# Thirty-four narrow unread matmuls in three waits of TensorE, and the two copies of a partial sum traded between ScalarE and VectorE

## The chip, the core and the metric

The kernel is one program on one NeuronCore of a Trainium2 chip. The metric is device microseconds from the start to the end of one execution, as median over several. TensorE (PE in the profile) multiplies into PSUM, VectorE (DVE) and ScalarE (ACT) read PSUM and write SBUF, GpSimd (POOL) works on SBUF and issues the weight loads, SyncE (SP) issues the other loads and the stores. The engines run their own instruction lists in order and meet only through semaphores.

## The reference

Two layers follow each other. The first is a gated recurrence over 5056 tokens for 4 sequences (B) and 256 channels (D); the second is a mixture of 8 experts with 4 slots each, over all 20224 tokens.

```
sig = 1 / (1 + exp(-f_logit));  f = lb + (1 - lb) * sig;  i = 1 - f
for t in range(S):  h = f[:, t] * h + i[:, t] * x[:, t];  y[:, t] = h

logits = y @ phi                                   # 20224 x 32 slots
d = exp(logits), divided by its sum over the tokens
slot_input = d.T @ y                               # 32 x 256
slot_out = relu(slot_input @ w1[e]) @ w2[e]        # each expert its 4 slots, F = 1024
c = exp(logits), divided by its sum over the slots
out = c @ slot_out
```

Nothing of `out` can be computed before `slot_out`, and `slot_out` needs all tokens and all weights.

## The kernel before

**First stage.** The tokens are cut into groups of 512 (`n_grp` = 10), and a unit `n` (0 to 39) is one group of one sequence. For each unit the tokens are loaded (`load`, SyncE), the gate is computed (`gate`, ScalarE, L235), gate times input is formed (`enter`, GpSimd, L246), both are transposed to channels by TensorE (`s_to_channels`, `u_to_channels`, L261, L267, and L255 and L258 for the odd group), the decay is made by ScalarE (`decay`, L295, L302), the recurrence is run by VectorE (`scan`, L313, two instructions a unit), the result is transposed back (`to_tokens`, L326) and copied out of PSUM by VectorE or ScalarE (`keep_tokens`, L345). Per group the logits are formed (`logits`, L359), exponentiated (`exps`, L368), transposed (`weights_to_tokens`, L380, copied by L383) and multiplied with the tokens into the sum `slot_ps` (`slots`, L410).

**Order.** The order of the work is written out by hand: the loop over `n` (L461 to L567) emits each unit's steps, and each engine runs its own in that order. GpSimd also issues the loads of the weights (`load_w`, L137 and L147) at the units that `W_AT` names, in program order behind its own work.

**Fillers.** `idle(k)` (L177) emits `k` float32 matmuls into `slot_bank[:, 1]`, the second half of the PSUM bank whose first half is `slot_ps`. Nothing reads that half. `spin(dst, k, w)` (L150) does the same with bfloat16 operands. At units 35 and 36 (`n_unit - 5`, `n_unit - 4`) there are `idle(2)` calls; unit 37 has none.

**Second stage.** `slot_ps` is copied out (L587), scaled to `sin` (L602, L603), goes through the first weights (L621) and ReLU (L626, L628), is transposed (L636) and laid into `hid` and `wide` (L645, L653), and goes through the second weights: experts 0 to 3 in L658, experts 4 to 7 in the loop over `j` and `fc` at L702, eight matmuls (L705) an expert. GpSimd clears `wide` (L572) before L653 writes it. The last expert's weights (`w_t`, tile of `w2_sb[7]`) come in three pieces: `fc` 0 to 3, 4 and 5, 6 and 7.

**The partial sum.** The sum over all but the last four `fc` of the last expert is kept in `so_ps`, the rest in `sb_ps`. When `so_ps` is complete, it is scaled and copied twice: to bfloat16 (`part_b`, ScalarE, L712) and to float32 (`part`, VectorE, L713). `part_b` feeds two matmuls of `early_part` (L699), which stand on TensorE between `fc` 5 and `fc` 6; their sums `early_ps` give the first two rows of the output of one sequence (`early`, L734) without waiting for `slot_out`. `part` is added to the rest in one VectorE instruction that makes `slot_out`:

```
nc.vector.scalar_tensor_tensor(slot_out, sb_ps, rcs, part, ALU.mult, ALU.add)
```

**Third stage.** All output tokens are formed from `slot_out` (L755) or its two-sequence form `slot_bd` (L738, L811), scaled by VectorE (L745) and ScalarE (L749), and stored by SyncE (L736, L785, L802, L817, L834).

Of the kernel before, what the change touches and what calls it, by code (L numbers as in the profile page):

```python
# [13 lines left out]
ACT = mybir.ActivationFunctionType  # L14
# [4 lines left out]
def kernel(  # L19
# [10 lines left out]
    nc = tc.nc  # L30
    B, S, D = x.shape
    E = moe_w1.shape[0]
    F = moe_w1.shape[2]
    NS = moe_phi.shape[1]
# [7 lines left out]
    n_unit = n_grp * B  # L42
# [27 lines left out]
    ident = consts.tile([P, P], BF16, name="ident")  # L70
# [13 lines left out]
    def rep_constants(b):  # L84
        blk = ident_f[ds(b * NS, NS), ds(b * NS, NS)]
        nc.gpsimd.tensor_copy(rep[ds(b * NS, NS)], blk.unsqueeze(1).broadcast_to([NS, B, NS]))  # L86
# [45 lines left out]
    w1_sb = [wts.tile([P, DC, F], BF16, name=f"w1_sb{e}") for e in range(E)]  # L132
# [29 lines left out]
    with tc.tile_pool(name="sp2", bufs=3) as sp2, \  # L162
# [9 lines left out]
        slot_bank = pslot.tile([P, 2, D], F32, name="slot_ps")  # L172
# [4 lines left out]
        def idle(k, first=False):  # L177
            if first:
                for i in range(2):
                    nc.tensor.matmul(slot_bank[:, 1, ds(0, P)], ident, ident,  # L180
                                     start=True, stop=False, skip_group_check=True)
            for _ in range(k):
                nc.tensor.matmul(slot_bank[:, 1], ident_f, wide_rep,  # L183
                                 start=False, stop=False, skip_group_check=True)
        xs, fs, sts, uts, pss, psus, hs, hps, hts, lgs, ets = ({} for _ in range(11))

        def long(n):
# [81 lines left out]
        def s_to_channels(n):  # L269
            if n % 2 == 0:  # L270
                pss[n // 2] = psp.tile([P, 2, P, R], F32, name="sp", tag="sp")
            to_channels(n, pss[n // 2][:, n % 2], sts[n // 2][:, n % 2],
                        sts[n // 2][:, 0, R3])
# [142 lines left out]
        def unit(f, m):  # L416
            if 0 <= m < n_unit:
                f(m)
# [60 lines left out]
        for n in range(n_unit):  # L479
            if n < SINGLE - 2:  # L480
                if n:
                    unit(to_tokens, n - 1)
                    unit(u_to_channels, n + 1)
                s_to_channels(n + 2)
                if n + 3 < SINGLE:
                    gate(n + 3, 1)
                decay(n + 2, 1)
                if n + 3 == SINGLE:
                    gate(n + 3)
                if n % 2 == 0:  # L490
                    unit(load, n + AHEAD)
                unit(enter, n + 3)
                rep_constants(n)
            else:
                end = n >= n_unit - 6
                if n % 2 == 0:
                    unit(load, n + AHEAD)
                    if n == SINGLE - 2:
                        to_tokens(n - 1)
                        keep_tokens(n - 1)  # L500
                    if not end and n >= SETTLED:
                        unit(gate, n + 4)
                else:
                    unit(decay, n + 1)
                    if n < SETTLED:
                        gate(n + 3)
                    if n == n_unit - 5:
                        gate(n + 3)
                        exps(odd - 1)
                if not end and n != n_unit - 7:  # L510
                    group(exps, n - 2)

                unit(enter, n + 3)
                for _ in range(W_AT.get(n, 0)):
                    load_w(w_next[0])
                    w_next[0] += 1

                if n == n_unit - 2:
                    unit(u_to_channels, n + 1)
                if n != SINGLE - 2:  # L520
                    unit(to_tokens, n - 1)
                if n == n_unit - 2:
                    keep_tokens(n - 1)
                if n % 2 == 0:
                    unit(s_to_channels, n + 2)
                    unit(s_to_channels, n + 3)
                if n != n_unit - 2:
                    unit(u_to_channels, n + 1)
                if n in (n_unit - 5, n_unit - 4):
                    idle(2)  # L530
                elif n == SINGLE - 2:
                    idle(1, True)
                elif n < n_unit - 4 and n % (2 * B) in (1, 5, 6, 7):
                    idle(2 if n in (6, 7) else 1)
                if n == n_unit - 2:
                    tail = psp.tile([P, 2, G], F32, name="tail", tag="sp")
                    sums = tail[:, 0]
                    rs_ps = sums[:, ds(0, n_grp * R * B)].rearrange(
                        "p (q b) -> p q b", b=B)
                    late_ps, odd_ps = (  # L540
                        tail[:, 1].bitcast(BF16)[:, ds(i * R * P, R * P)].rearrange(
                            "p (r s) -> p r s", r=R) for i in range(2))
                    logits(odd)
                    exps(odd)
                    slots(odd - 2)
                elif not end and long(n - 1):
                    if n % B == 0:
                        g = (n - 1) // (2 * B) * 2
                        for i in range(2):
                            logits(g + i, [2, 3] if n % (2 * B) == 0 else [0, 1])  # L550
                elif not end:
                    group(logits, n - 1)
            if n == n_unit - 1:
                odd_weights()
                logits(last, [0, 1, 2])

            unit(scan, n)
            if n not in (SINGLE - 2, n_unit - 2):
                unit(keep_tokens, n - 1)
            if n == n_unit - 3:  # L560
                weights_to_tokens(odd - 1, nc.scalar.copy)
            elif not n >= n_unit - 6:
                group(weights_to_tokens, n - 3)
                batch(slots, n - 4, 0)
                batch(slots, n - 4, 1)
                if n > 2 * B and n % (2 * B) == 3:
                    idle(1)  # L567
# [22 lines left out]
        for o in range(DC):  # L590
            nc.tensor.matmul(sin_ps[:, o], slot_v[:, o], rep[:, 0],
                             start=True, stop=True, skip_group_check=True)
        spin(slot_bank[:, 1], 6, D)

    with tc.tile_pool(name="ew", bufs=1) as ew, \
# [18 lines left out]
        for q in range(E // Q):  # L614
            hi = ew.tile([P, F], BF16, name=f"hi{q}")
            for k in range(2):
                hi_ps = (psu.tile([P, H], F32, name="hi_ps", tag="up") if q == 0 else
                         pbig.tile([P, H], F32, name="hi_ps", tag=f"hi_ps{k}"))
                for o in range(DC):
                    for j in range(Q):  # L620
                        nc.tensor.matmul(hi_ps[ds(j * NS, NS)], sin[:, o],  # L621
                                         w1_sb[q * Q + j][:, o, ds(k * H, H)],
                                         start=(o == 0), stop=(o == DC - 1),
                                         skip_group_check=True)
# [6 lines left out]
        rcs = ew.tile([P, 1], F32, name="rcs")  # L631
# [24 lines left out]
        for e in range(Q):  # L656
            for fc in range(FC):
                nc.tensor.matmul(so4_ps[ds(fc % 4 * NS, NS), :], hid[:, fc, e],  # L658
                                 w2_sb[e][:, fc],
                                 start=(e == 0 and fc < 4),  # L660
                                 stop=(e == Q - 1 and fc >= FC - 4),
                                 skip_group_check=True)
# [10 lines left out]
        so_ps = pm.tile([P, D], F32, name="so_ps", tag="pm")  # L673
# [3 lines left out]
        for i in range(0, n_late, 2):  # L677
            g_ps = psu.tile([P, 2, 2, P], F32, name="g_ps", tag="up")
            for k in range(2):
                nc.tensor.matmul(g_ps[:, k], hi_v[tail_b, FC - n_late + i + k], ex[tail_b],  # L680
                                 start=True, stop=True, skip_group_check=True)
            nc.scalar.copy(gs[:, ds(i, 2)].rearrange("p k r t -> p (k r t)"),
                           g_ps.rearrange("p k r t -> p (k r t)"))
        part = ew.tile([P, D], F32, name="part")
        part_b = ew.tile([P, D], BF16, name="part_b")
# [16 lines left out]
        for j in range(Q):  # L702
            for fc in range(FC):
                late = j == Q - 1 and fc >= FC - n_late
                nc.tensor.matmul(sb_ps if late else so_ps,  # L705
                                 wide[:, fc, j].rearrange("p b s -> p (b s)"),
                                 w2_sb[Q + j][:, fc],
                                 start=(j == 0 and fc == 0) or (late and fc == FC - n_late),
                                 stop=j == Q - 1 and fc in (FC - n_late - 1, FC - 1),
                                 skip_group_check=True)  # L710
                if j == Q - 1 and fc == FC - n_late - 1:
                    nc.scalar.activation(part_b, so_ps, ACT.Copy, scale=rcs)  # L712
                    nc.vector.tensor_scalar_mul(part, so_ps, rcs)  # L713
                if j == Q - 1 and fc == FC - 3:
                    early_row(0, 0, 2)
                    early_part(0)
                    early_part(1)
            if j == 0:
                nc.tensor.matmul(so_ps, rep2, so4, start=False, stop=False,
                                 skip_group_check=True)  # L720
                row_sums(1)
            if j == 1:
                row_sums(2)
                spin(unread, 4, D)
                q = n_grp * R - 1
                nc.vector.reciprocal(rrow[:, wide_r:q], rs_ps[:, wide_r:q])
                nc.vector.reciprocal(rrow[:, q, ds(0, B // 2)], rs_ps[:, q, ds(0, B // 2)])
# [5 lines left out]
        for r in range(2):  # L733
            nc.scalar.activation(early[:, r], early_ps[r], ACT.Copy,  # L734
                                 scale=rrow[:, r, ds(B - 1, 1)])
# [140 lines left out]
```

## Time and profile before

| | us |
|---|---|
| median of 3 runs | 197.88 |
| lowest and highest | 197.66, 198.44 |
| the profiled execution, as timed | 198.21 |
| its span in the profile | 196.4 |

The profiled execution's own time lies 1.81 us above its span and 0.33 us above the median. Its mean granted TensorE clock is 0.866 of full speed.

| engine | busy us | share of the span |
|---|---|---|
| PE | 149.9 | 76% |
| DVE | 144.1 | 73% |
| ACT | 142.6 | 73% |
| POOL | 103.3 | 53% |

Times in the profile count from the start of the span. A row of the timeline has start, length, engine, source line, operation, output and inputs, shapes, count, and in brackets how long the engine was idle before it and what released it. The ends of matmuls are modelled. In the chain that ended last a row has start, length and what the time was spent on. The page's slices cut the span into 40 equal parts of 4.91 us.

### The profile page before, as it was taken

How to read it: one execution, taken by the hardware profiler on the slowest of the kernel's cores; microseconds unless marked ns; L12 is line 12 of the kernel's file. 1: busy time of each engine (PE TensorE's matmuls, PEld its weight loads, DVE VectorE, ACT ScalarE, POOL GpSimd, SP SyncE). 2: the span in 40 equal slices, each digit the busy share in tenths (PEclk: the TensorE clock that was granted, in tenths of full speed). 3: DMA queues.
4: the chain of work that ended last, by engine and by line, in shares of the span. 5: the costliest groups of instructions: out<-in, count | busy, mean ns of one | idle time of the engine just before them, and what ended most of it. 6: DMA issues, size and time to landing. Idle time of an engine off the chain costs nothing.

```text
span 196.4 us, 3258 instructions
## 1 busy us (share of the span) xinstructions
PE 149.9 (76%) x1196; PEld 105.8 (54%) x1196; DVE 144.1 (73%) x185; ACT 142.6 (73%) x201; POOL 103.3 (53%) x78
## 2 busy tenths in 40 slices
PE   0687579789979979897998888999889999920000
PEld 0475458577766858665776766668664434300000
DVE  2669789998799999999999999343277988920000
ACT  3688778899699998999998797334089999950000
POOL 2689586894988588894969976291030000000000
PEclk9999999996999999999999999999995555555555
DMA  6999999999999999999999999999749999999994
GB/s 205 420 422 418 430 430 420 427 425 333 405 427 424 398 343 422 427 417 308 405 419 385 259 222 214 214 214 213 138 162 432 422 432 424 427 427 437 444 444 173
DMA packets 14161, 70.75 MB, mean 360 GB/s; under 512 B 1585, under 2 KB 2866, under 8 KB 10178
## 3 DMA queue, kind: packets, MB, share of 16 engines
q1 hardware_dynamic: 11520, 62.13, 76.5%
q0 software_dynamic: 2624, 8.42, 21.5%
q8 instruction: 9, 0.15, 0.3%
q14 instruction: 6, 0.05, 0.1%
q10 hardware_dynamic: 2, 0.00, 0.0%
HBM read 58.23 MB, written 20.71 MB: 402 GB/s over the span
## 4 chain that ended last, share of the span: by engine, by line
DMA 37%; PE 25%; DVE 13%; ACT 5%; POOL 4%; issue 4%; ACTq 0%; SPq 0%; POOLq 0%
DMA x_t<-in_x_dram 14%; DVE h L313 10%; PE op L811 8%; DMA w_t<-in_moe_w_dram 8%; DMA f_t<-in_f_logit_dram 7%; DMA w_sb<-in_moe_w_dram 7%; POOL u_t L246 4%; PE hp L326 4%; ACT oc L749 3%; PE up L267 3%; DVE ht L345 3%; PE sp L261 2%; PE op L755 2%; PE lg L359 1%; PE slot_ps L183 1%
## 5 line engine op out<-in xcount | busy, mean ns | idle before, releaser
L246 POOL TENSOR_TENSOR u_t<-s_t,x_t 128x1024 bf16<-128x1024 bf16 (+1 forms) x39 | 82.5, 2131 | 21.8 <-ACT s_t L235 12.3
L313 DVE TENSOR_TENSOR_SCAN h<-a,h,up 128x512 bf16<-128x512 f32 (+1 forms) x72 | 86.9, 1253 | 3.9 <-PE up L267 2.6
L235 ACT ACTIVATE s_t<-f_t 128x2048 bf16<-128x2048 f32 (+2 forms) x23 | 38.4, 1669 | 7.1 <-DMA f_t<-in_f_logit_dram 7.1
L326 PE MATMUL hp<-ident_f,h 128*128 128x128 f32 (+1 forms) x160 | 29.4, 308 | 8.0 <-DVE ht L345 5.8
L326 PEld LDWEIGHTS hp<-ident_f,h 128*128 128x128 f32 (+1 forms) x160 | 23.4, 207 | 18.7 <-DVE ht L345 10.9
L261 PE MATMUL sp<-ident_f,s_t 128*128 128x128 f32 x144 | 21.3, 291 | 6.8 <-ACT s_t L235 4.5
L295 ACT ACTIVATE a<-sp,lbs 128x1024 f32<-128x1024 bf16 x24 | 25.5, 1117 | 0.6 <-PE sp L261 0.6
L749 ACT ACTIVATE oc<-op,rrow 128x256 f32<-128x256 f32 x62 | 24.5, 508 | 0.2
L811 PE MATMUL op<-slot_bd,etall 64*128 64x512 bf16 x62 | 23.6, 594 | 0.4 <-POOL slot_bd L738 0.3
L261 PEld LDWEIGHTS sp<-ident_f,s_t 128*128 128x128 f32 x144 | 17.4, 150 | 8.7 <-ACT s_t L235 5.0
L745 DVE TENSOR_TENSOR oc<-op,rrow 128x512 f32<-128x512 f32 x31 | 20.0, 685 | 2.0 <-PE op L811 1.9
L302 ACT ACTIVATE a<-sp,lbs 128x512 f32<-128x512 bf16 (+2 forms) x22 | 17.8, 857 | 3.8 <-PE sp L261 3.5
L267 PE MATMUL up<-ident_f,u_t 64*128 64x64 f32 x192 | 17.6, 229 | 2.4 <-POOL u_t L246 2.4
L183 PE MATMUL slot_ps<-rep,ident_f 128*128 128x256 f32 x52 | 17.0, 422 | 1.0 <-POOL rep L86 1.0
L267 PEld LDWEIGHTS up<-ident_f,u_t 64*128 64x128 f32 x192 | 13.9, 138 | 6.3 <-POOL u_t L246 2.8
L811 PEld LDWEIGHTS <-etall 64*128 64x128 bf16 x62 | 9.2, 155 | 13.5 <-issue 7.8
L345 DVE COPY ht<-hp 128x512 f32<-128x512 f32 (+1 forms) x20 | 13.4, 670 | 1.4 <-PE hp L326 1.4
L345 ACT COPY ht<-hp 128x512 f32<-128x512 f32 (+1 forms) x20 | 11.7, 583 | 3.5 <-PE hp L326 3.4
L313 DVE TENSOR_TENSOR_SCAN h<-a,up 128x512 bf16<-128x512 f32 x8 | 9.3, 1207 | 2.5 <-PE up L261 2.5
L183 PEld LDWEIGHTS slot_ps<-rep,ident_f 128*128 128x128 f32 x52 | 8.3, 193 | 3.0 <-POOL rep L86 1.2
L359 PE MATMUL lg<-h,phi 128*32 128x512 bf16 (+1 forms) x80 | 9.4, 389 | 0.3 <-ACT et L383 0.2
L261 PE MATMUL up<-ident_f,u_t 128*128 128x128 f32 x48 | 8.9, 314 | 0.5 <-POOL u_t L246 0.5
(126 smaller groups left out, 150.3 us busy)
## 6 DMA issues: line engine op xcount, KB each, us to landing
f_t<-in_f_logit_dram SPq DMA_DIRECT2D x12, 1024.0 KB, 13.3
x_t<-in_x_dram SPq DMA_DIRECT2D x12, 1024.0 KB, 12.0
out_dram<-oc SPq DMA_DIRECT2D x6, 2048.0 KB, 13.7
w_sb<-in_moe_w_dram POOLq DMA_DIRECT2D x14, 512.0 KB, 11.1
f_t<-in_f_logit_dram SPq DMA_DIRECT2D x12, 512.0 KB, 8.4
x_t<-in_x_dram SPq DMA_DIRECT2D x12, 512.0 KB, 9.9
out_dram<-oc SPq DMA_DIRECT2D x4, 896.0 KB, 6.3
out_dram<-ob SPq DMA_DIRECT2D x1, 2048.0 KB, 9.8
```

The lines of the kernel that those rows point to most:

```text
L183: nc.tensor.matmul(slot_bank[:, 1], ident_f, wide_rep, start=False, stop=False, skip_group_check=True)
L235: nc.scalar.activation(s_t, f_t, ACT.Sigmoid, scale=-1.0)
L246: nc.gpsimd.tensor_tensor(uts[n][:, :r], s_t[:, :r], x_t[:, :r], ALU.mult)
L261: nc.tensor.transpose(ps[:, :, r], t[:, r], ident_f)
L267: nc.tensor.transpose(v[:, :, r], t(r)[k].bitcast(F32), ident_f[k, k])
L295: nc.scalar.activation(a, sp[:, :, :, :, o], ACT.Identity, scale=nomlb[:, ds(o, 1)], bias=1.0)
L313: nc.vector.tensor_tensor_scan(h[:, :T, o], decays[n // 2, o][:, n % 2, :T], up[:, :T, o], hs[number(g - 1, b)][:, ds(used(g - 1) - 1, 1), ...
L326: nc.tensor.transpose(hp[:n_p, r], hw[:, :n_p, r], ident_f)
L345: copy(hts[g][:n_p, b].rearrange("p r d -> p (r d)").bitcast(F32), hps.pop(n)[:n_p].rearrange("p r c -> p (r c)"))
L745: nc.vector.tensor_tensor(ob, op, scale.broadcast_to(list(ob.shape)), ALU.mult)
L749: nc.scalar.activation(ob[:, i], op[:, i], ACT.Copy, scale=scale[:, i])
L811: nc.tensor.matmul(op.rearrange("p u d -> p (u d)"), ew[:, :, r], slot_bd[ds(j * 2 * NS, 2 * NS)].rearrange("s u d -> s (u d)"), start=Tru ...
```

## The change

A helper `narrow(k)` is added beside `idle`. It emits `k` bfloat16 matmuls whose stationary operand is 32 columns of the identity and whose moving operand is 256 columns of the first expert's first weights (`w1_sb[0]`, loaded long before); they go round the four groups of 32 partitions of `slot_bank[:, 1]`, which nothing reads. Units 35 and 36 get 12 of them each, behind `idle(2)`, and unit 37 gets 10, where there was no filler.

The two copies of the partial sum trade engines and order: VectorE makes the bfloat16 `part_b` first, ScalarE makes the float32 `part` after it.

```diff
+        def narrow(k):
+            for i in range(k):
+                b = ds(i % B * NS, NS)
+                nc.tensor.matmul(slot_bank[b, 1], ident[:, b], w1_sb[0][:, 0, ds(0, D)],
+                                 start=False, stop=False, skip_group_check=True)
...
                 if n in (n_unit - 5, n_unit - 4):
                     idle(2)
+                    narrow(12)
+                elif n == n_unit - 3:
+                    narrow(10)
                 elif n == SINGLE - 2:
                     idle(1, True)
...
                 if j == Q - 1 and fc == FC - n_late - 1:
-                    nc.scalar.activation(part_b, so_ps, ACT.Copy, scale=rcs)
-                    nc.vector.tensor_scalar_mul(part, so_ps, rcs)
+                    nc.vector.tensor_scalar_mul(part_b, so_ps, rcs)
+                    nc.scalar.activation(part, so_ps, ACT.Copy, scale=rcs)
```

On TensorE the 34 matmuls with their 34 weight loads stand, in three blocks, ahead of the transposes of L326 of unit 35's turn and unit 36's turn, and between the transposes of L261 and L380 of unit 37's turn. Nothing else on TensorE moves. On VectorE and ScalarE the order of all other instructions is kept. Some waits change: `part_b` now waits for TensorE directly on VectorE; `part` waits for VectorE on ScalarE; the first matmul of `early_part` waits for VectorE; and `slot_out`, which waited first for VectorE's own `part` and then for TensorE, now waits first for TensorE, in an instruction of its own, and then for ScalarE's `part`. ScalarE's `early` no longer waits for VectorE.

## Prediction

> **What bounds the kernel now.** I read the slices of the page first, then the chain that ended last, then the timeline round the places that the change touches, and last the rows by stretch for the clock.
>
> The two rows of slices are the granted TensorE clock and the share of the 16 DMA engines that is busy:
>
> ```profile
> PEclk9999999996999999999999999999995555555555
> DMA  6999999999999999999999999999749999999994
> ```
>
> The DMA engines are full from the second slice through the 28th and again from the 31st on. The first stretch is the loading of 58 MB, the second the storing of 20.7 MB. Only the two slices between (the 29th and 30th, 7 and 4 tenths, 137.5 to 147.3 us) are not full. So the end is set by loads, then a short chain of compute, then stores. The chain says the same:
>
> ```profile
> 125.11 16.37 DMA w_t<-in_moe_w_dram
> 141.47 0.04 issue
> 141.52 0.39 PE sb_ps L705 x2
> 141.91 0.22 PE early_ps L694 x2
> 142.13 0.27 PE early_ps L699 x2
> 142.40 0.22 PE sb_ps L705 x2
> 142.62 0.23 PE early_ps L694 x2
> 142.85 0.12 issue
> 142.97 0.49 DVE slot_out L728
> ```
>
> In the rows ahead of these the chain is on other weights (w_sb) from 111.90 to 124.82, so from 111.90 to 141.47 it is nothing but weights on their way. The reader is to see that the three filler places (111 to 119 us) lie inside that stretch, off the chain, while the trade of the two copies lies on it, in the 1.5 us from 141.47 to 142.97.
>
> The timeline of TensorE round the three places:
>
> ```profile
> 113.29 0.70 PE L326 MATMUL hp<-ident_f,h 128*112 128x128 f32 x4 [0.75 <-DVE ht L345]
> ...
> 116.95 0.75 PE L326 MATMUL hp<-ident_f,h 128*128 128x128 f32 x4 [0.51 <-ACT ht L345]
> ...
> 119.45 0.75 PE L326 MATMUL hp<-ident_f,h 128*128 128x128 f32 x4 [0.34 <-ACT ht L345]
> ...
> 120.75 0.62 PE L410 MATMUL slot_ps<-ht,et 128*32 128x256 bf16 x16
> 121.30 0.75 PE L326 MATMUL hp<-ident_f,h 128*128 128x128 f32 x4
> ```
>
> There are three waits, 0.75, 0.51 and 0.34 us, each ahead of L326 and each for a copy on another engine; the first two follow the `idle` matmuls of L183. And the timeline of ScalarE and VectorE at the partial sum:
>
> ```profile
> 141.50 0.47 ACT L712 ACTIVATE part_b<-so_ps,rcs 128x256 bf16<-128x256 f32 x1 [5.84 <-PE so_ps L705]
> 142.01 0.48 DVE L713 TENSOR_SCALAR part<-so_ps,rcs 128x256 f32<-128x256 f32 x1 [2.64 <-ACT part_b L712]
> 142.97 0.48 DVE L728 SCALAR_TENSOR_TENSOR slot_out<-sb_ps,rcs,part 128x256 bf16<-128x256 f32 x1 [0.48 <-PE early_ps L694]
> 142.88 0.91 ACT L734 ACTIVATE early<-early_ps,rrow 128x256 f32<-128x256 f32 x2 [0.90 <-PE early_ps L694]
> ```
>
> **The fillers.** A narrow matmul has the form of L410: 128 rows, 32 columns, 256 bfloat16 columns moving, going round the four column groups. Sixteen of those start at 120.75 and the next work starts at 121.30, so one costs 0.55 / 16 = 34 ns. Twelve cost 0.41 us, ten 0.34.
> - Unit 35: 0.41 in a wait of 0.75 for VectorE's copy. Hidden, with 0.34 to spare.
> - Unit 36: 0.41 in a wait of 0.51 for ScalarE's copy. Hidden, with 0.10 to spare. If that cover went, L326 would be late, then the transposes at 117.54 behind it, then VectorE's scan at 118.24, which waited only 0.17 for them.
> - Unit 37: the ten stand ahead of the eight L380 at 117.97 and the four L261 at 118.45. Both move by 0.34. The copy of L380's result (ScalarE, L383) starts at 119.26, when ScalarE is free; the transposes that are 0.34 later would be done at 118.92. The scan behind the four L261 starts only after another unit's scans. The next thing on TensorE, L326 at 119.45, had waited 0.34 for ScalarE. Hidden, with nothing to spare.
>
> The wait they carry, for the weights of the first expert, ended tens of us before. No queue of SyncE or GpSimd is passed: GpSimd's own work and its weight loads wait for gates and for buffers, not for these transposes. So the fillers cost nothing. Behind them there is more cover: TensorE waits 0.53 us for weights before L705 at 139.56 and 0.21 before L705 at 140.80, together 0.74, and ScalarE waits 1.24 for GpSimd to clear `wide`.
>
> The granted clock was 1.00 in every us from 100 to 147, so in this execution there is no half clock for the fillers to prevent, and their gain is nothing too.
>
> **The trade, up to `early_part`.** L705's last matmul into `so_ps` ends at 140.80 + 0.60 = 141.40. ScalarE started 0.10 later, behind a wait instruction of its own. VectorE will wait in the instruction itself; L587, which waits so, started 0.05 after the end of L455. So `part_b` runs from 141.45, takes 0.48 as L713 did from the same bank (output type aside), and is there at 141.93 in place of 141.97. TensorE is through L694 at 141.75 + 2 x 0.11 = 141.97 and started L699 at 142.02. The gain is 0.05 us for everything behind it. The last piece of weights has to be there too: its last landing is at 142.10, ahead of the 142.19 at which `fc` 6 would start.
>
> **The trade, `slot_out`.** ScalarE's `part` starts at about 142.02 and takes 0.47, so it is there at 142.50, as before (142.49), and ahead of TensorE's sum. What changes is which wait stands in a separate instruction. Before, VectorE's wait instruction for `part` ran at 142.53, and L728 started 0.44 us later; after, the wait instruction is for `sb_ps`, which ends at 142.62 before and 142.57 now. No row shows this instruction after that wait, so it is bounded. If L728 needs 0.44 after any wait instruction, it starts at 142.57 + 0.04 + 0.44 = 143.05: 0.08 later than now. If what held it was the write of `part` on its own engine, it starts as other VectorE work does behind a wait instruction (L442 and L646, 0.04 to 0.05 after): at 142.67, 0.30 earlier. I take +0.05, near the row of this very instruction, and keep -0.30 and +0.08.
>
> From `slot_out` on, everything is pushed by the same amount: DMA is at 0.09, 0.42 and 0.39 of its capacity from 143 to 146, so stores start when they can.
>
> **The sum.** 0 for the fillers, -0.05 and +0.05 for the trade: 0.0 us. On the profiled execution that is 198.2; this execution stood 0.33 above the median, so on the median it is 197.9.
>
> **Rivals.**
>
> *The clock gate (faster).* The rows by stretch show one drop of the clock:
>
> ```profile
> 44.00:45.00 1.00, 0.54 (x8) 0.45 (x12) 1.00 (x2) 1.00 (x1) 0.41 (x1) 0.96 0.99 418
> 45.00:46.00 1.00, 1.00 (x17) 0.52 (x10) 1.00 (x2) 0.99 (x2) 0.00 (x0) 0.50 0.99 348
> ```
>
> The clock is halved from 44.96 to 48.4, some 3.4 us, behind a wait of 0.91 us of TensorE. In that time L410's sixteen took 1.03 against 0.62, L183's two 1.22 against 0.70, L326's four 1.06 against 0.75 and L261's eight 1.36 against 1.04: 1.6 us more. If in most executions such a drop falls between 112 and 125, and the fillers prevent it, they save 1.6 less the cover of 0.74, so 0.9 us: 197.0. For it: three waits that total 1.60 us in 7. Against it: the clock stayed at 1.00 there, and also over the wait of 1.16 us at 103. The Trainium skill, page "TensorE: Matmul & The Clock Gate", Part 1, says that activity is judged in free-running windows of 3413 ns; the length of the drop agrees, and by that rule the place of the drop would change between executions, which one profile cannot show. It decides if the drop comes in more than half of the executions. Chance 0.17, of it 0.14 by over 0.5%.
>
> *Code loading (slower).* The queue q8 moves 9 packets of 16 KB of instructions, one per some 266 of the 2392 loads and matmuls of TensorE. They start at 107.6, 124.4, 134.6 and 143.7 us and take 0.94 to 0.96 us of one DMA engine. The last one comes after the weights. With 68 more instructions ahead of it, it comes when TensorE is 68 instructions less far: not at 143.7 but between 138 and 142, while the last weights land. If it falls on a DMA engine that is among the last to land, the piece of `fc` 6 and 7 is late by up to 0.96, less the 0.14 between its landing (142.10) and its use (142.24): +0.8, so 198.7. Against it: the sixteen landings of that piece spread from 140.23 to 142.10, and seven of them lie over 0.9 us ahead of the last. It decides if the engine is one of the other nine. The Trainium skill, page "Runtime: NRT & Kernel Launch", Instruction fetch mechanics, calls the cost of crossing a 16 KiB block mostly hidden; by that this rival is worth 0. Chance 0.14, of it 0.06 by over 0.5%, with the +0.08 of `slot_out` on top.
>
> *Fillers longer than their waits (slower).* If they do not overlap as L410 does but cost 0.11 each as L705 does, they take 1.3, 1.3 and 1.1 us, and TensorE is late by 0.55 + 0.79 + 0.74 = 2.1, less 0.74 of cover: 1.3, so 199.2. It begins at 43 ns each (0.51 / 12). Against it: the same form at 34 ns. Chance 0.09, of it 0.06 by over 0.5%.
>
> **How the numbers follow.** A measurement of this kernel tells about 0.5%, 1.0 us, from no change. My forecast has 0.60, between 197.5 and 198.3 (the ends of `slot_out`, and the 0.3 between executions). With the rivals: faster by over 0.5% 0.14, slower 0.06 + 0.06 = 0.12, within 0.74. The range reaches to the clock gate's 197.0 and past code loading's 198.7, to 198.8.
>
> **What the profile after would show.** The waits before L326 shrunk to some 0.3, 0.1 and 0, with the releasers unchanged and the scans at the same times; L705's waits for `w_t` still there at 139.6 and 140.8; the last w_t landing near 142.1; `part_b` on VectorE done before 142.0; `slot_out` between 142.7 and 143.1. Wrong would be: L326's wait gone and the scan of 118.24 late; no wait before L705; a q8 packet ahead of 142 with the last landing later; or a clock under 1.00 between 100 and 147.

## The result, and the profile after

| | median us | lowest to highest | runs |
|---|---|---|---|
| before, beside it | 197.96 | 197.63 to 198.44 | 15 |
| changed | 198.89 | 197.94 to 199.38 | 15 |

The changed kernel takes 1.0040 of the time before (95% interval 1.0026 to 1.0054): slower by some 0.8 us by that ratio (the two medians lie 0.93 apart), with 1 outside the interval, and less than the 0.5% that the prediction named. The forecast was 197.9 with 198.8 as the upper end; 1.0040 of the median of 197.88 that it started from is 198.7. That was the price of the rival "code loading", and code loading is what happened.

The profiled execution took 198.47 us, with a span of 196.7 (before: 198.21 and 196.4). Its slices:

```profile
PEclk9999958979999999999999999999995555555555
DMA  5999999999999999999999999999749999999994
```

The DMA row is that of before, to one tenth in the first slice. The clock row is not: before, the clock was halved once ahead of the stores, for 3.4 us. Here, by the rows by stretch, it is halved for 6.8 us from about 24 and for 3.4 us from about 41 (sixth to ninth slices), in units that the change does not touch, and TensorE reaches the first filler place's L326 at 115.47 in place of 113.29. Of the fifteen timed executions, five had a mean granted clock of 0.848 or 0.849, this one among them, and took 198.37 to 198.49. Nine had 0.850 to 0.874 and took 198.65 to 199.38. (One, at 0.856, took 197.94.) The kernel before also has executions at 0.847 to 0.849: 11 of the 83 that were timed beside the experiments below, at 198.15 to 198.85 with a median of 198.42. So at that clock the two kernels take the same time. The page of the changed kernel shows the less common of its two ways to run, one without the loss, and the loss has to be sought in another execution (the last experiment below).

The chain that ended last, round the partial sum, in this execution:

```profile
140.36 0.46 PE unread L152 x4
140.82 1.32 PE so_ps L715 x12
142.14 0.02 issue
142.16 0.49 DVE part_b L722
142.66 0.04 issue
142.70 0.38 PE early_ps L709 x2
143.08 0.22 PE sb_ps L715 x2
143.30 0.23 PE early_ps L704 x2
143.53 0.24 issue
143.77 0.49 DVE slot_out L738
```

Before, a weight load ended at 141.47 and released TensorE. Here no load stands in the rows: TensorE runs from one matmul to the next, because compute is late and the weights are there already (the piece that `sb_ps` starts with landed by 141.49). `slot_out` starts at 143.77 in place of 142.97.

The timeline of TensorE at the three filler places (L189 are the narrow matmuls, L333 is L326 of before):

```profile
114.66 0.51 PE L189 MATMUL slot_ps<-w_sb,ident 128*32 128x256 bf16 x12
115.47 0.70 PE L333 MATMUL hp<-ident_f,h 128*112 128x128 f32 x4 [0.30 <-DVE ht L352]
118.55 0.51 PE L189 MATMUL slot_ps<-w_sb,ident 128*32 128x256 bf16 x12
119.13 0.75 PE L333 MATMUL hp<-ident_f,h 128*128 128x128 f32 x4
120.24 0.51 PE L189 MATMUL slot_ps<-w_sb,ident 128*32 128x256 bf16 x10
121.62 0.62 PE L333 MATMUL hp<-ident_f,h 128*128 128x128 f32 x3
```

The starts of the three L333 are 3.66 and 2.49 us apart. Before, they were 3.66 and 2.50 apart (113.29, 116.95, 119.45). The waits of 0.75, 0.51 and 0.34 us have shrunk to 0.30 and nothing, and the distances have not grown: the fillers are as long as the waits allow.

VectorE and ScalarE at the traded copies:

```profile
142.16 0.48 DVE L722 TENSOR_SCALAR part_b<-so_ps,rcs 128x256 bf16<-128x256 f32 x1 [1.01 <-PE so_ps L715]
142.74 0.47 ACT L723 ACTIVATE part<-so_ps,rcs 128x256 f32<-128x256 f32 x1 [5.17 <-DVE part_b L722]
143.77 0.48 DVE L738 SCALAR_TENSOR_TENSOR slot_out<-sb_ps,rcs,part 128x256 bf16<-128x256 f32 x1 [1.13 <-PE early_ps L704]
143.55 0.91 ACT L744 ACTIVATE early<-early_ps,rrow 128x256 f32<-128x256 f32 x2 [0.34 <-PE early_ps L704]
```

### The profile page after: what moved, and what is told of

Read it like the earlier page. It is cut to its first block, busy times and chain, and to the rows that moved or that the text cites. A ratio compares the mean times of both kernels' runs of the same rounds, so it can differ in the third digit from the quotient of the medians.

```text
span 196.7 us, 3326 instructions
## 1 busy us (share of the span) xinstructions
PE 153.1 (78%) x1230; PEld 108.0 (55%) x1230; DVE 144.1 (73%) x185; ACT 142.6 (72%) x201; POOL 103.2 (52%) x78
## 4 chain that ended last, share of the span: by engine, by line
PE 34%; DVE 16%; DMA 14%; ACT 11%; issue 6%; POOL 6%; POOLq 1%; ACTq 0%; SPq 0%; DVEq 0%
DMA x_t<-in_x_dram 14%; DVE h L320 12%; PE op L821 9%; POOL u_t L253 5%; PE hp L333 4%; DVE ht L352 3%; PE up L274 3%; ACT oc L759 3%; ACT s_t L242 3%; PE sp L268 3%; PE op L765 2%; ACT a L309 2%; PE so_ps L715 2%; PE lg L366 1%; PE slot_ps L183 1%
## 5 line engine op out<-in xcount | busy, mean ns | idle before, releaser
L333 PE MATMUL hp<-ident_f,h 128*128 128x128 f32 (+1 forms) x160 | 29.8, 312 | 8.1 <-DVE ht L352 7.6
L333 PEld LDWEIGHTS hp<-ident_f,h 128*128 128x128 f32 (+1 forms) x160 | 23.8, 207 | 19.0 <-DVE ht L352 13.6
L268 PE MATMUL sp<-ident_f,s_t 128*128 128x128 f32 x144 | 21.9, 296 | 7.0 <-ACT s_t L242 4.7
L183 PE MATMUL slot_ps<-rep,ident_f 128*128 128x256 f32 x52 | 17.8, 439 | 0.5 <-POOL rep L86 0.5
L268 PE MATMUL up<-ident_f,u_t 128*128 128x128 f32 x48 | 9.5, 330 | 0.7 <-POOL u_t L253 0.6
```

What stands on the lines that cost most here:

```text
L183: nc.tensor.matmul(slot_bank[:, 1], ident_f, wide_rep, start=False, stop=False, skip_group_check=True)
L268: nc.tensor.transpose(ps[:, :, r], t[:, r], ident_f)
L333: nc.tensor.transpose(hp[:n_p, r], hw[:, :n_p, r], ident_f)
```

## The experiments

Three theories were to be told apart. **A, code loading:** 68 more TensorE instructions move the last 16 KB packet of code ahead in time, from behind the weights into their last landings. **B, the trade:** the copies on other engines make `slot_out` late. **C, the fillers as work:** they make TensorE late at 111 to 122 us. The instruction packets of queue q8 are taken from the trace's own packet records; the landings are the sixteen semaphore updates of each piece of `w_t`. The trace does not say which DMA engine a landing belongs to. "Piece 2" is `fc` 4 and 5, for which TensorE waits ahead of the first matmul into `sb_ps`; piece 3 is `fc` 6 and 7. The first runs shared the runs of the kernel before: 198.03 us (31 runs).

### The trade alone

```diff
-                    nc.scalar.activation(part_b, so_ps, ACT.Copy, scale=rcs)
-                    nc.vector.tensor_scalar_mul(part, so_ps, rcs)
+                    nc.vector.tensor_scalar_mul(part_b, so_ps, rcs)
+                    nc.scalar.activation(part, so_ps, ACT.Copy, scale=rcs)
```

> The trade of the two copies alone, no narrow matmuls. Theory A (code loading: the 68 more TensorE instructions bring the last 16 KB code packet of q8 ahead of 142 us, among the last weights): nothing of the loss, +0.1 us (the wait instruction ahead of slot_out), 0.0 to +0.2, and the last q8 packet near 143.7 as before. Theory B (the trade itself lengthens the chain from so_ps to slot_out): all of the loss, +0.8 us. Theory C (the fillers make TensorE late at 111 to 122 us): nothing, 0.0.

Measured: 197.96 us (11 runs), ratio 0.9995 (0.9981 to 1.0009). Without the fillers the trade costs nothing that can be measured, so B alone falls. The last code packet starts at 143.10, piece 2 lands by 141.32.

### The fillers alone

```diff
                     idle(2)
+                    narrow(12)
+                elif n == n_unit - 3:
+                    narrow(10)
```

> The 34 narrow matmuls alone, at their places, the copies as before. Theory A: +0.7 to +0.8 us, the last q8 packet between 138 and 142. Theory B: 0.0. Theory C: +0.7 to +0.8, with the waits before the transposes of h (L326 before) gone.

Measured: 198.63 us (8 runs), ratio 1.0039 (1.0025 to 1.0052): the whole loss of the change to within the intervals. The chain of waits of this kernel:

```profile
124.97 17.71 DMA w_t<-in_moe_w_dram
142.68 0.05 issue
142.73 0.39 PE sb_ps L715 x2
143.12 0.22 PE early_ps L704 x2
```

and its group of the matmuls into `sb_ps` (count, busy time and mean ns of one, idle time before them and what ended it):

```profile
L715 PE MATMUL sb_ps<-w_t,wide 128*128 128x256 bf16 x4 | 0.8, 276 | 1.5 <-DMA w_t<-in_moe_w_dram 1.5
```

The load ends at 142.68 where it ended at 141.47 before, and TensorE waits 1.5 us for it where it waited 0.1. Fifteen of the sixteen landings of piece 2 are there by 141.35, as before; the sixteenth comes 1.33 later. The last code packet starts at 140.67 and takes 0.975 us of one DMA engine. `slot_out` starts at 143.81.

### The same 34, a hundred microseconds earlier

```diff
                 elif n == SINGLE - 2:
                     idle(1, True)
+                    narrow(34)
```

Here the moving operand is the identity (128 columns), since the first weights are not loaded yet at unit 4.

> The same 34 narrow matmuls, copies as before, but all 34 at unit 4 (about 20 us), with the identity as moving operand (128 columns in place of 256). The code is as many instructions longer ahead of the weights' end, the three waits at 111 to 119 us are left as they were. Theory A: +0.7 to +0.8 us, as in the run with the 34 at their places. Theory B and theory C: 0.0 (0.2 either way).

Measured: 198.73 us (12 runs), ratio 1.0031 (1.0017 to 1.0045). The loss is the same with the 34 at 26 us and the three waits at 111 to 119 left as they were. C falls: it is the number of instructions ahead of the last weights that counts, not where they stand. The packet starts at 140.30, the last landing of piece 2 is at 142.43, and TensorE waits 1.3 us for it.

### Twelve fillers

```diff
                     idle(2)
+                    narrow(4)
+                elif n == n_unit - 3:
+                    narrow(4)
```

> Only 4 narrow matmuls at each of the three places, 12 in place of 34, copies as before. The code is 24 instructions longer in place of 68. Theory A: the last q8 packet moves by about 1.5 us, to 142 or later, behind the last landing; 0.0 us, not a third of the loss. Theory C: a third of the loss or less, 0.0 to +0.3. Theory B: 0.0.

Measured: 197.65 us (11 runs), ratio 0.9982 (0.9974 to 0.9991). With 24 more instructions the packet starts at 141.63, when piece 2 (141.35) is there and piece 3 (141.98) nearly. TensorE waits 0.1 us. The same kernel later gave 197.75 us (12 runs) against 198.07 (29 runs), ratio 0.9994 (0.9983 to 1.0005):

> The 12 narrow matmuls with the copies as before once more, on the chip of the other two runs. Theory A: -0.3 to -0.4 us, as the first time. Rival (chance of the first time): 0.0.

So this is no loss for certain, and a gain of 0.3 us in both medians but only in one of the two intervals.

What this kernel may gain is to be seen on SyncE. The rows of the two stores of `early` (number; shortest, median and longest issue in ns; first and last start), first of before, where the last packet starts at 143.74, then of this kernel:

```profile
L736 SPq DMA_DIRECT2D out_dram<-early x2: 347/788/1228, 143.4 to 143.9; - x2
```

```profile
L746 SPq DMA_DIRECT2D out_dram<-early x2: 348/364/381, 143.3 to 143.7; - x2
```

The second issue took 1228 ns before, 1139 with the trade alone (packet at 143.10), and 377 to 387 in the four first kernels whose packet came ahead of 142 with the copies as before (34, 34 early, 24 and 12 fillers). The first store of `ob` is issued behind it, at 145.18 before and 144.59 here. That the packet holds the issue up is what the coincidence suggests; no run took it apart.

### The changed kernel again, and twelve fillers with the trade

A second profile of the changed kernel:

> The changed kernel once more, for a second profile, since the first one had its compute late for another reason. Theory A: where TensorE is in time for the weights (a wait for w_t before the matmuls into so_ps at 140.6 or so), the last q8 packet starts between 139 and 141.5, the slowest of the sixteen DMA engines lands the last piece of w_t near 142.9 in place of 142.1, and slot_out starts at 143.6 to 143.9. Where TensorE is late, as in the first profile, the packet comes behind the weights and nothing of this shows.

It took 198.12 us, again at a clock of 0.848, with drops from the sixth slice on; its packet came at 141.46 and its weights were on time, `slot_out` at 143.41. It repeats the page and shows no loss either: the kernel before took 198.00 beside it (23 runs), and 198.15 in the one of them at 0.849.

Twelve fillers and the trade together, twice:

> The change with 4 narrow matmuls at each of the three places in place of 12, 12 and 10: both parts of the change, 24 instructions instead of 68. Theory A: -0.3 us, as with the 12 alone, and at most 0.1 from the wait instruction ahead of slot_out: -0.4 to -0.2. Theory B (the trade costs where nothing else hides it): -0.1 or above.

> The 12 narrow matmuls with the trade once more, beside the 12 without. If the trade costs by the wait instruction ahead of slot_out: 0.1 us slower than the 12 with the copies as before. If the 0.3 between their first runs is the trade: 0.3 slower. If that was chance: the same.

Measured: 197.92 us (12 runs), ratio 0.9998 (0.9988 to 1.0009), and 197.78 us (12 runs), ratio 0.9994 (0.9982 to 1.0005). The first pair, 197.65 without and 197.92 with the trade, looked like a cost of 0.3 us; the second pair, 197.75 and 197.78 on one chip, does not repeat it. In the chain of undisturbed executions the trade does cost something: from the start of the first L694 to `slot_out` it takes 142.97 - 141.75 = 1.22 us before and 142.90 - 141.60 = 1.30 with the trade. That is 0.08, too little for these runs.

### Twenty-four and sixty fillers

```diff
                     idle(2)
+                    narrow(8)
+                elif n == n_unit - 3:
+                    narrow(8)
```

> 8 narrow matmuls at each place, 24 in all, 48 instructions, copies as before. Theory A: the last q8 packet starts between those of the run with 12 (141.6) and of the run with 34 (140.7), so near 141.1, while one DMA engine still has its last piece to move: +0.3 to +0.8 us. If the loss grows with the fillers themselves, it is two thirds of that of 34: +0.4; the two then differ in the landings alone.

Measured: 198.68 us (12 runs), ratio 1.0019 (0.9996 to 1.0043), but in groups: four runs at 197.66 to 197.81, one at 198.18, four at 198.68 to 198.80, and three at 200.17 to 201.46. The profiled one is of the group round 198.7 (198.69): packet at 140.69, piece 2 at 142.70, TensorE waiting 1.3 us. So the loss is there or not, about 1 us, and does not grow with the number. What the three above 200 are stays open; none was profiled.

```diff
                     idle(1, True)
+                    narrow(60)
```

> 60 narrow matmuls at unit 4 in place of 34, copies as before, 120 instructions longer. The last q8 packet comes near 137 to 138, with four more us of weights behind it. Theory A: the DMA engine that carries it stays late by the packet's 0.9 us to the end, so the loss is that of 34 early ones, +0.5 to +0.8. Rival: only a packet among the last pieces hurts, since an engine catches up over 4 us: 0.0.

Measured: 199.64 us (6 runs), ratio 1.0086 (1.0067 to 1.0105): +1.6 us where 0.5 to 0.8 was expected. A miss in size. The packet starts at 138.07, while the weights of the expert ahead of the last are landing. From then on one landing of each load is late by some 1 us: of that expert's weights (the first half of the tile `w_t`) fifteen land by 139.44 and the sixteenth at 140.41, and the sixteenths of the three pieces come at 141.72, 142.34 and 142.96. It reads as one DMA engine that was made late and did not catch up before its queue ran dry. On top, a tenth packet of code falls into the stores (166.6), and in the profiled execution, the slowest of the six, the clock is halved round 142 (a first pair into `sb_ps` takes 0.53 in place of 0.39). How the extra 0.8 splits between these was not measured.

### Both copies on VectorE, with twelve fillers

```diff
                     idle(2)
+                    narrow(4)
+                elif n == n_unit - 3:
+                    narrow(4)
...
-                    nc.scalar.activation(part_b, so_ps, ACT.Copy, scale=rcs)
+                    nc.vector.tensor_scalar_mul(part_b, so_ps, rcs)
                     nc.vector.tensor_scalar_mul(part, so_ps, rcs)
```

> 4 narrow matmuls at each place, and VectorE makes both copies, part_b first, so that the wait instruction ahead of slot_out is again for VectorE's own part and the wait for TensorE is in slot_out itself. Theory A, with the wait instruction as the only cost of the trade: as fast as 12 narrow matmuls with the copies as before, or 0.05 us faster, so -0.3 to -0.4 against the kernel before, and 0.1 to 0.3 faster than the 12 with the trade. If VectorE's reading of the partial sum is what costs: as slow as the 12 with the trade.

Measured: 197.51 us (12 runs) against 198.07, ratio 0.9978 (0.9966 to 0.9990). It beats both kernels, and is the best seen here; against twelve fillers alone on the same chip (0.9994, 0.9983 to 1.0005) the intervals still touch. The timeline of VectorE:

```profile
141.44 0.48 DVE L722 TENSOR_SCALAR part_b<-so_ps,rcs 128x256 bf16<-128x256 f32 x1 [1.94 <-PE so_ps L715]
141.84 0.48 DVE L723 TENSOR_SCALAR part<-so_ps,rcs 128x256 f32<-128x256 f32 x1
142.61 0.48 DVE L738 SCALAR_TENSOR_TENSOR slot_out<-sb_ps,rcs,part 128x256 bf16<-128x256 f32 x1 [0.30 <-PE sb_ps L715]
```

`slot_out` starts 0.02 us after the end of the second pair into `sb_ps` (142.59 by the chain), 0.36 earlier than before. That the wait for `part` is over early does not explain this. VectorE's wait instruction ends at 142.37 here, only 0.24 us ahead of `slot_out`; in each of the other 13 profiles 0.41 us or more lie between the two. One more thing differs. In those 13 an 8 KB code packet on queue q14 starts 1.06 to 1.10 us after the wait instruction, wherever that falls (142.37 to 143.87). Here, with one more VectorE instruction ahead of that point, it starts at 135.87, and the gap is gone. So the gap fits a fetch of VectorE's own code between the two instructions better than it fits the form of the wait. No run moves VectorE's code alone, so that cause is not shown.

### The changed kernel, in an execution with the clock of before

> The changed kernel once more, for a profile of an execution whose mean granted clock is above 0.85; the two looked at so far had 0.848, were late in compute by other means, and took their last 16 KB packet at 141.5 to 141.6, behind the weights. Nine of the fifteen timed executions had 0.850 to 0.874 and took 198.65 to 199.38, above the others. Code loading (theory A) expects in such an execution what the run of the 34 matmuls alone showed: the last packet between 140.0 and 141.2, among the last weights; TensorE waiting 1.2 to 1.6 us for w_t ahead of the first matmul into sb_ps, which starts at 142.4 to 142.8; then slot_out 0.42 us behind its own wait instruction, so at 143.9 to 144.3 (143.81 with the copies as before, where it followed the end of sb_ps by 0.03); 198.8 to 199.2. If the weights land on time (wait under 0.3) in an execution at such a clock that takes over 198.7, theory A does not explain the upper group of the changed kernel's times. With a clock of 0.848 again, 198.1 to 198.5 and slot_out at 143.4 to 143.8, and nothing new is told.

Measured: 199.01 us beside 197.98 for the kernel before, span 197.2, clock 0.865. This is an execution of the group that shows the loss. The slices of TensorE's clock are those of before; the chain of waits:

```profile
125.14 17.58 DMA w_t<-in_moe_w_dram
142.72 0.05 issue
142.76 0.39 PE sb_ps L715 x2
143.16 0.22 PE early_ps L704 x2
143.37 0.22 PE early_ps L709 x2
143.59 0.22 PE sb_ps L715 x2
143.81 0.23 PE early_ps L704 x2
144.04 0.26 issue
144.30 0.49 DVE slot_out L738
```

its timeline of TensorE at the second stage's end:

```profile
139.59 1.03 PE L715 MATMUL so_ps<-w_t,wide 128*128 128x256 bf16 x8 [0.53 <-DMA w_t<-in_moe_w_dram]
140.84 0.60 PE L715 MATMUL so_ps<-w_t,wide 128*128 128x256 bf16 x4 [0.22 <-DMA w_t<-in_moe_w_dram]
142.76 0.39 PE L715 MATMUL sb_ps<-w_t,wide 128*128 128x256 bf16 x2 [1.33 <-DMA w_t<-in_moe_w_dram]
```

and at the filler places:

```profile
113.27 0.70 PE L333 MATMUL hp<-ident_f,h 128*112 128x128 f32 x4 [0.30 <-DVE ht L352]
...
116.92 0.75 PE L333 MATMUL hp<-ident_f,h 128*128 128x128 f32 x4
...
119.42 0.75 PE L333 MATMUL hp<-ident_f,h 128*128 128x128 f32 x4
...
121.27 0.75 PE L333 MATMUL hp<-ident_f,h 128*128 128x128 f32 x4
```

Up to 140.84 this execution is before's to within 0.04 us: the transposes behind the fillers start 0.03 earlier than the 113.29, 116.95, 119.45 and 121.30 of before, and both waits for the weights are there. Then one landing is missing. The last code packet starts at 140.71 and takes 0.974; fifteen landings of piece 2 are there by 141.51, the sixteenth comes at 142.72.

The account of this execution against the profiled one of before: the load ends 1.25 us later (142.72 against 141.47); `slot_out` starts 1.33 later (144.30 against 142.97); the first store of `ob` is issued 0.85 later (146.03 against 145.18), since the second store of `early` took 657 ns to issue, not 1228; the span is 0.8 longer (197.2 against 196.4). Theory A holds with all its numbers. B comes in through it: against the fillers alone, with the same late load (142.68), `slot_out` starts at 144.30 in place of 143.81, 0.49 later, and the span is 0.3 longer. The timed executions agree: the nine of the changed kernel at 0.850 to 0.874 have a median of 199.03, the eight with the fillers alone 198.63. So the trade, which costs nothing by itself, adds 0.3 to 0.4 us where the load is late.

## Why the prediction was wrong, point by point

- **"So the fillers cost nothing."** At their places, yes. L326 starts when it did, with 0.30 us of wait left at the first (predicted 0.34) and none at the second and third (0.10 and 0). One narrow matmul costs 44 ns, not 34: the ten of unit 37 start at 120.24 and the next work starts at 120.68, so 0.44 / 10. The rival of fillers longer than their waits set its beginning at 43; at 44 the delay is under what the rows show. As 68 instructions they cost the kernel its loss, and the forecast of 0.0 fell there. The step that failed is the weighing of the rivals: code loading got 0.14, less than the clock gate. That the measured time still lies at the upper end of the range is owed to a bound that was drawn past this rival, not to the sum of 0.0.
- **Code loading, "+0.8, so 198.7".** This is what decided, and the mechanism was right to the packet: last packet between 138 and 142 (140.71), some 1 us of one DMA engine (0.974), a landing late. What spoke against it was that seven of the sixteen landings lay over 0.9 us ahead of the last. In each profile where the packet started between 140.3 and 140.7 (34, 34 early and 24 fillers, and the changed kernel at 199.01) one landing of piece 2 came some 1.2 us after the other fifteen; in the nine where it started at 141.46 or later none did. And it struck piece 2, for which TensorE was already waiting, with nothing to spare, and not only piece 3 with its 0.14: the load ended 1.25 later. The 0.8 came out all the same, because the slow store issue of before (1228 ns) went away, and the trade added to it. The size was right by luck, through terms that were not in it. The Trainium skill, page "Runtime: NRT & Kernel Launch", Instruction fetch mechanics, has the 16 KiB blocks, and the packets of q8 agree (16,384 bytes); its "mostly hidden" fits the runs with none or twelve fillers, and not those with 34 (1.0039 alone).
- **The trade, up to `early_part`: 0.05 gained.** Right: from L694's start to `early_part` it took 0.27 us before and 141.82 - 141.60 = 0.22 with the trade alone.
- **The trade, `slot_out`: +0.05, between -0.30 and +0.08.** The upper bound was the measured one: with weights on time `slot_out` starts at 143.06 with twelve fillers and the trade, where that bound's working gave 143.05. Its reason, 0.44 "after any wait instruction", is too wide, since the gap was 0.24 with both copies on VectorE; and the other reading, the write of `part` on its own engine, is out, since with the trade alone the wait is for TensorE and the gap is 0.42 all the same. The sum was also wrong in form: the 143.05 had the gain of 0.05 in it already, so the trade should have stood at +0.05 to +0.08 and not at -0.05 + 0.05. The bound of +0.08 did not hold once the load was late (+0.49), because before, the wait instruction for `part` is over long before such a load ends, while after it the instruction waits for `sb_ps` itself.
- **"From `slot_out` on everything is pushed by the same amount."** Wrong. 1.33 us at `slot_out` became 0.85 at the first store of `ob` and 0.8 at the end; in the profiled execution at the lower clock 0.80 became 0.3 of span. The issue of the stores before had a delay of its own, which the change removed.
- **The clock gate.** The clock does drop in some executions: twice early in the changed kernel's page, and five of its fifteen executions share that clock. But in the two profiles at that clock the drops come between 24 and 52 us, far ahead of the fillers, not between 112 and 125, where the fillers could have prevented them. (The drop before begins at 44.92, not 44.96: a mean of 0.96 with half the clock leaves 0.08 us. Nothing hangs on it.) In the execution at 199.01 the clock is 1.00 from 110 to 147.
- **The profile after.** Of the signs named, "a q8 packet ahead of 142 with the last landing later" is the one that came true; it was named as what would be wrong.

## What to carry to other kernels

Instructions that fit into a wait are free on their engine and are still code: where the DMA queues are full and a load ends the chain, look at when the engine's code packets fall, before and after, and move the count of instructions (here by 24 rather than 68) to put the packet where nothing lands. If a rival's mechanism meets a place without slack on the chain, don't let a spread of landings talk its chance down: with 60 fillers the lateness lasted through four loads. Look at the code of the other engines too; the gap of 0.42 or 0.24 us ahead of `slot_out` hints at VectorE's, which was not tested. And take a second profile when the times of one kernel fall into groups: the first may show the group that is not the loss.

## What the runs showed of the hardware that was not expected

- A 16 KB code packet took 0.88 to 0.98 us of one DMA engine in most cases (1.01 to 1.33 for the last packet in four profiles). Where it fell among the last weights, one landing in sixteen was about 1.2 us late (142.72 after 141.51); with the packet at 138.07, four loads in a row had one late landing.
- The second of two small store issues on SyncE took 1228 and 1139 ns with a 16 KB code packet under way, 344 to 387 in the seven profiles with fillers and without the trade's order of engines, 448 to 657 in the five with the trade and fillers. Why those five lie between is not known.
- `slot_out`, a SCALAR_TENSOR_TENSOR, starts 0.41 us or more after the separate wait instruction ahead of it on VectorE in 13 profiles, 0.24 in the one whose q14 packet comes early, and 0.02 to 0.04 after the wait that it holds itself where that ends last. Which of two waits becomes the separate instruction, set here by the engines of the two copies, was worth 0.49 us with late weights (143.81 against 144.30).
